# First batch of an attention and MLP kernel: squares in pairs, an earlier first k, and the last chunks divided anew

## Chip, cores, metric

One core of a Trainium2 chip. The metric is device time in microseconds (us) of that core. The trace's span is shorter than the time: by 2.1 us in the kernel before (399.3 and 401.45 for its profiled run).

## The reference

```python
# q, k, v: (8 batches, 12 heads, 448, 64) f32
scores = scale * q @ k^T;  attn = maximum(scores, 0)**2 / 448;  a = attn @ v
x = a.transpose(0, 2, 1, 3).reshape(3584, 768)
h = x @ w_in                                    # 768 x 2048
out = (maximum(h, 0) + alpha * minimum(h, 0)) @ w_out   # 2048 x 768
```

Attention without a softmax, then an MLP. The engines are called PE (TensorE, matmuls), DVE (VectorE), ACT (ScalarE) and POOL (GpSimd); PSUM is where this kernel's matmuls put their results. The kernel takes four heads at a time as a group: 24 groups n, three to a batch, each in 7 chunks j of scores.

## The kernel before

A chunk has score matmuls into PSUM (tile sc, two halves of one tile; or sch, two tiles), a relu to bf16 (rl) and a square on DVE (at). Attention times v (av) needs all 7 chunks of its group; its result is evicted to xT. The MLP runs as 16 ff chunks of 6 "hps" matmuls, an ACT and a DVE operation that writes gT, then "ops" matmuls with w_out. Batch 0 runs ahead of everything; from there the attention of later batches is spread between the MLP's matmuls, so that PE has no gap.

```python
for n in range(NG):                      # batch 0
    last = n == NG - 1
    for j in range(NJ):
        if j == 2 or (j == 5 and not last): scores(n, j, "both", mm_ps)
        else: scores(n, j, "both" if j == 6 and last else "act")
        squares(keep=1)
        if j == 2 and n > 0: attnv(n - 1, space=mm_ps)
        if j == 3 and not last: transpose(n + 1, "k")
        if j == 4 and not last: transpose(n + 1, "q")
        if last and j >= 4: ffn1(0, j - 4, range(0, 4))
    if n == 0:                           # the load queue, issued from POOL
        load_bf16(2)                     # k, q, v of group 2
        load_w_in(0, 512); load_w_in(512, 1024); load_w_in(1024, 2048)
        load_bf16(3)
# ... half of w_out, group 4, half of w_out ...
attnv(2, range(0, 4)); ffn1(0, 3, range(0, 4)); squares(both=True); attnv(2, range(4, NJ))
# ... beta from alpha ...
for ff in range(4): ffn1(0, ff, range(4, KM))
play([f[4], f[5], turn(3), f[6], f[7], (3, 0), f[8], ...])  # f[i]: ff chunk i; turn(3): transposes of k and q of group 3
```

```python
def group(units, phase):                 # the stream: up to three chunks of later groups
    def f():
        # ... scores of each unit, attnv ...
        squares()
        for n, j in units_:
            # ... at j == 0: load(n + 2), transpose k and q of n + 1 ...
            if j == 4 and n + 2 < NQ:
                for w in "kqv": to_bf16(n + 2, w, nc.gpsimd)   # POOL casts f32 -> bf16
    return f
```

## Time and profile before

| | before |
|---|---|
| time, four runs | 401.09 us median (400.79 to 401.98) |
| PE busy, share of the chain | 97%, 92% |
| start of the fifth ff chunk ("f4") | 33.68 us |
| transposes of q of group 3, landing of that q | 36.45 us, 34.93 us |
| first ops matmul | 50.54 us |

PE is nearly always busy, so one reads where it is not: ahead of f4. The prediction shows those lines. One more view: the loads that POOL issues. It is the issue list, cut to the issue of q of group 3; the last number is us from issue to landing.

```profile
qe<-in_q_dram POOLq DMA_DIRECT2D x1, 224.0 KB, 11.1
```

### The profile page before, as it was taken

The numbers are of one execution on the slowest core, as the hardware profiler recorded it, in microseconds if no ns is written. First come the engines' busy times: TensorE is split into PE (matmuls) and PEld (weight loads), VectorE is DVE, ScalarE is ACT, GpSimd is POOL, SyncE is SP. The second block draws the span as 40 slices with busy tenths as digits, with TensorE's granted clock in tenths as the row PEclk, the third lists the DMA queues.
The fourth block names the chain that finished last, engine by engine and source line by source line (L and its number), as shares of the span: only waits on it lengthen the run. The fifth ranks groups of instructions, "written<-read, shape, count | busy, mean of one in ns | idle before, by whom it ended". The sixth has DMA issues, their size and how long they took to land.

```text
span 399.3 us, 7923 instructions
## 1 busy us (share of the span) xinstructions
PE 387.3 (97%) x3201; PEld 200.8 (50%) x3201; DVE 258.1 (65%) x411; ACT 221.0 (55%) x345; POOL 72.8 (18%) x88
## 2 busy tenths in 40 slices
PE   8788999999999999999999999999999999999995
PEld 5434455444555445544555455554555445555562
DVE  3775767768664877567665777768575776736411
ACT  5785754788544766456544775656464585624200
POOL 6564000022021430033020360033002300000000
PEclk9699999999999999999999999999999999999999
DMA  6999995494098933393097961295058720130033
GB/s 145 189 209 205 203 250 204 116 242 150 21 244 202 252 136 80 86 270 100 2 215 197 250 192 43 64 274 155 2 144 187 200 48 0 41 79 2 0 80 79
DMA packets 64164, 55.44 MB, mean 139 GB/s; under 512 B 35696, under 2 KB 59776, under 8 KB 64128
## 3 DMA queue, kind: packets, MB, share of 16 engines
q1 hardware_dynamic: 53152, 44.98, 43.7%
q0 software_dynamic: 10976, 9.96, 15.6%
q8 instruction: 25, 0.41, 0.4%
q14 instruction: 11, 0.09, 0.1%
HBM read 45.62 MB, written 11.01 MB: 142 GB/s over the span
## 4 chain that ended last, share of the span: by engine, by line
PE 92%; DVE 2%; DMA 2%; ACT 1%; issue 1%; POOL 0%; ACTq 0%
PE ops L247 38%; PE hps L231 35%; PE av L202 7%; PE sc L159 6%; PE sch L159 4%; DMA qe<-in_q_dram 2%; DVE at L184 1%; PE tps L134 1%; DMA qraw<-in_q_dram 1%; PE avh L202 1%; ACT rl L173 0%; DVE gT L239 0%; ACT xT L211 0%; ACT xT L217 0%; POOL ke L103 0%
## 5 line engine op out<-in xcount | busy, mean ns | idle before, releaser
L247 PE MATMUL ops<-w_out_sb,gT 128*128 128x384 bf16 x896 | 153.4, 327 | 0.0
L231 PE MATMUL hps<-xT,w_in_sb 128*128 128x448 bf16 x768 | 151.2, 353 | 1.4 <-ACT xT L211 0.5
L184 DVE TENSOR_TENSOR at<-rl 128x896 bf16<-128x896 bf16 x167 | 111.1, 685 | 19.0 <-ACT rl L173 8.8
L247 PEld LDWEIGHTS <-gT 128*128 128x128 bf16 x896 | 84.1, 98 | 67.2 <-issue 14.7
L231 PEld LDWEIGHTS <-w_in_sb 128*128 128x128 bf16 x768 | 73.1, 98 | 75.7 <-issue 10.2
L239 DVE SCALAR_TENSOR_TENSOR gT<-neg,beta_sb,hps 128x448 bf16<-128x448 f32 x128 | 83.9, 677 | 35.7 <-ACT neg L238 35.1
L173 ACT ACTIVATE rl<-sc 128x896 bf16<-128x896 f32 x109 | 95.8, 927 | 7.7 <-PE sc L159 5.3
L238 ACT ACTIVATE neg<-hps 128x448 f32<-128x448 f32 x128 | 68.4, 553 | 55.0 <-PE hps L231 52.9
L255 DVE COPY osb<-ops 128x384 f32<-128x384 f32 x56 | 31.1, 555 | 54.5 <-PE ops L247 54.5
L109 POOL CAST kb<-kraw 128x896 bf16<-128x896 f32 x16 | 16.2, 1011 | 210.0 <-DMA kraw<-in_k_dram 210.0
L165 ACT ACTIVATE rl<-sch 128x448 bf16<-128x448 f32 x37 | 20.1, 544 | 56.4 <-PE sch L159 56.4
L159 PE MATMUL sc<-qT,kT 64*64 64x448 bf16 x464 | 36.4, 362 | 2.7 <-ACT rl L173 2.2
L202 PE MATMUL av<-at,vb 64*64 64x448 bf16 x616 | 33.1, 350 | 0.0
L166 DVE TENSOR_SCALAR rl<-sch 128x448 bf16<-128x448 f32 x37 | 23.0, 620 | 14.1 <-PE sch L159 14.1
L159 PEld LDWEIGHTS <-kT 64*64 64x64 bf16 x672 | 14.9, 106 | 29.6 <-issue 25.0
L202 PEld LDWEIGHTS <-vb 64*64 64x64 bf16 x672 | 20.3, 110 | 13.2 <-issue 1.4
L169 ACT ACTIVATE rl<-sch 128x448 bf16<-128x448 f32 x30 | 14.6, 544 | 16.9 <-PE sch L159 16.9
L217 ACT ACTIVATE xT<-av 128x896 bf16<-128x896 f32 x21 | 19.4, 922 | 6.8 <-PE av L202 6.7
L159 PE MATMUL sch<-qT,kT 64*64 64x448 bf16 x208 | 20.3, 380 | 0.0
L109 POOL CAST qb<-qraw 128x896 bf16<-128x896 f32 x16 | 18.4, 1151 | 0.0
L109 POOL CAST vb<-vraw 128x896 bf16<-128x896 f32 x16 | 16.8, 1053 | 1.4 <-DMA vraw<-in_v_dram 0.8
L171 DVE TENSOR_SCALAR rl<-sc 128x896 bf16<-128x896 f32 x6 | 6.5, 1084 | 2.9 <-PE sc L159 2.9
(47 smaller groups left out, 72.6 us busy)
## 6 DMA issues: line engine op xcount, KB each, us to landing
out_dram<-osb SPq DMA_DIRECT2D x56, 192.0 KB, 2.8
qraw<-in_q_dram SPq DMA_DIRECT2D x19, 448.0 KB, 4.6
kraw<-in_k_dram SPq DMA_DIRECT2D x19, 448.0 KB, 5.3
vraw<-in_v_dram SPq DMA_DIRECT2D x18, 448.0 KB, 6.3
w_out_sb<-in_moe_w_out_dram POOLq DMA_DIRECT2D x2, 1536.0 KB, 19.8
w_in_sb<-in_moe_w_in_dram POOLq DMA_DIRECT2D x8, 192.0 KB, 8.2
w_in_sb<-in_moe_w_in_dram POOLq DMA_DIRECT2D x4, 384.0 KB, 9.7
vb<-in_v_dram POOLq DMA_DIRECT2D x6, 224.0 KB, 9.9
```

Of the source, the lines that this page charges most:

```text
L109: eng.tensor_copy(o, i)
L159: nc.tensor.matmul(half[r][64 * c:64 * c + 64, :S], kT[n][64 * r:64 * r + 64, j, c, :], qT[n][64 * r:64 * r + 64, :, c, :], start=True, st ...
L165: nc.scalar.activation(rl[:, 0], half[0][:, :S], ACTF.Relu)
L166: nc.vector.tensor_scalar(rl[:, 1], half[1][:, :S], 0.0, None, ALU.max)
L173: nc.scalar.activation(rl, ps[:, :, :S], ACTF.Relu)
L184: nc.vector.tensor_tensor(a, rl, rl, ALU.mult)
L202: nc.tensor.matmul(half[r][64 * s:64 * s + 64, :S], vb[n][64 * r:64 * r + 64, s, j, :], a[64 * r:64 * r + 64, s], start=(j == 0), stop=(j ...
L231: nc.tensor.matmul(ps, w_in_sb[:, km // 2, km % 2, bass.ts(ff, 128)], xT[b][:, km // 2, km % 2, :], start=(km == 0), stop=(km == KM - 1))
L238: nc.scalar.activation(neg, ps, ACTF.Relu, scale=-1.0)
L239: nc.vector.scalar_tensor_tensor(gT[b // 2][:, ff, (b % 2) * S:(b % 2) * S + S], neg, beta_sb[:, ff:ff + 1], ps, ALU.mult, ALU.add)
L247: nc.tensor.matmul(ps, gT[sb][:, ff, bass.ts(c, 128)], w_out_sb[:, ff, bass.ts(hf, 384)], start=(ff == 0), stop=(ff == KF - 1))
L255: nc.vector.tensor_copy(o[:, bass.ts(hf, 384)], ps)
```

## The change

The intent is to start the dense stream sooner: fewer DVE operations in batch 0, first scores earlier, and a tail in which ACT and DVE work side by side.

```diff
-    g_pool = pool("g", 2)
+    g_pool = pool("g", 1)                    # makes room for the pair tiles
+    def squares2(keep=0):                    # one DVE operation on two chunks (128x1792)
+        while len(todo) >= 2 + keep: ...
+            nc.vector.tensor_tensor(a, t, t, ALU.mult)
@@ attention times v
+            elif apart:                      # two PSUM tiles, not two halves of one
+                av_ps[n] = [sc_ps.tile([128, 2, 512], ...)[:, 0] for _ in range(2)]
-            if g == NG - 1:
+            if g > 0:                        # second half of xT on DVE for groups 1 and 2
@@ first loads: k in two transfers
+    for js in (first, rest):                 # chunks 0-2, then 3-6
+        nc.sync.dma_start(out=raw[(0, "k")][:, :, lo:hi]..., in_=...)
-    warm(4)
     transpose(0, "k", first, nc.scalar)
     warm(2)
+    scores(0, 0, pair=True); scores(0, 1, pair=True); scores(0, 2, "both", mm_ps, pair=True)
     transpose(0, "k", rest)
@@ chunk loop
-                scores(n, j, "both" if j == 6 and last else "act")
+                scores(n, j, "dve" if last and j == 4 else "act", pair=True)
-            squares(keep=1)
+                squares2(keep=1)
@@ tail
-    attnv(2, range(0, 4)); ffn1(0, 3, range(0, 4)); squares(both=True); attnv(2, range(4, NJ))
+    squares(eng=nc.scalar)                   # the last chunk alone, on ACT
+    attnv(2, range(0, 4), apart=True); attnv(2, range(4, NJ)); ffn1(0, 3, range(0, 4))
```

The turning of alpha into beta also moves from the tail to the end of group 0.

More of the change, by code (lines that the diff above doesn't have):

```diff
@@ L59 @@
     at_pool = pool("at", 10)
+    rl2_pool = pool("rl2", 3)
+    at2_pool = pool("at2", 6)
     xT_pool = pool("xT", 2)
-    g_pool = pool("g", 2)
+    g_pool = pool("g", 1)
     neg_pool = pool("neg", 3)
@@ L148, with score_tile, score_mm @@
     att, xT, todo = {}, {}, []
-    def scores(n, j, relu="act", space=sc_ps):
+    def score_tile(space=sc_ps):
         if space is mm_ps:
-            half = [mm_ps.tile([128, 512], F32, tag="mm", name="sch") for _ in range(2)]
-        else:
-            ps = sc_ps.tile([128, 2, 512], F32, tag="sc", name="sc")
-            half = [ps[:, r] for r in range(2)]
-        for r in range(2):
+            return None, [mm_ps.tile([128, 512], F32, tag="mm", name="sch") for _ in range(2)]
+        ps = sc_ps.tile([128, 2, 512], F32, tag="sc", name="sc")
+        return ps, [ps[:, r] for r in range(2)]
+    def score_mm(n, j, half, rs=range(2)):
+        for r in rs:
             for c in range(2):
@@ L162, in scores, with relu_half, relu_tile @@
                                  start=True, stop=True)
-        rl = rl_pool.tile([128, 2, S], BF16, tag="rl", name="rl")
-        if relu == "both":
-            nc.scalar.activation(rl[:, 0], half[0][:, :S], ACTF.Relu)
-            nc.vector.tensor_scalar(rl[:, 1], half[1][:, :S], 0.0, None, ALU.max)
-        elif relu == "act2":
-            for r in range(2):
-                nc.scalar.activation(rl[:, r], half[r][:, :S], ACTF.Relu)
+    def relu_half(rl, half, r, eng):
+        if eng is nc.scalar:
+            nc.scalar.activation(rl[:, r], half[r][:, :S], ACTF.Relu)
+        else:
+            nc.vector.tensor_scalar(rl[:, r], half[r][:, :S], 0.0, None, ALU.max)
+    rl2, pairs = [], []
+    def relu_tile(pair):
+        if not pair:
+            return rl_pool.tile([128, 2, S], BF16, tag="rl", name="rl")
+        if not rl2:
+            t = rl2_pool.tile([128, 2, 2, S], BF16, tag="rl2", name="rlp")
+            rl2.extend([t, t])
+            pairs.append(t)
+        t = rl2.pop()
+        return t[:, 1 - len(rl2)]
+    def scores(n, j, relu="act", space=sc_ps, pair=False):
+        ps, half = score_tile(space)
+        score_mm(n, j, half)
+        rl = relu_tile(pair)
+        if relu in ("both", "act2"):
+            relu_half(rl, half, 0, nc.scalar)
+            relu_half(rl, half, 1, nc.vector if relu == "both" else nc.scalar)
         elif relu == "dve":
@@ L174, in scores, with squares @@
         todo.append((n, j, rl))
-    def squares(keep=0, both=False):
+    def squares2(keep=0):
+        while len(todo) >= 2 + keep:
+            two = [todo.pop(0) for _ in range(2)]
+            t = pairs.pop(0)
+            a = at2_pool.tile([128, 2, 2, S], BF16, tag="at2", name="atp")
+            nc.vector.tensor_tensor(a, t, t, ALU.mult)
+            for i, (n, j, _) in enumerate(two):
+                att[(n, j)] = a[:, i]
+    def squares(keep=0, eng=None):
         while len(todo) > keep:
@@ L179, in squares @@
             a = at_pool.tile([128, 2, S], BF16, tag="at", name="at")
-            if both:
-                nc.scalar.activation(a[:, 0], rl[:, 0], ACTF.Square)
-                nc.vector.tensor_tensor(a[:, 1], rl[:, 1], rl[:, 1], ALU.mult)
+            if eng is nc.scalar:
+                nc.scalar.activation(a, rl, ACTF.Square)
             else:
@@ L187, with attnv @@
     av_ps = {}
-    def attnv(n, js=range(NJ), space=sc_ps):
+    def attnv(n, js=range(NJ), space=sc_ps, apart=False):
         b, g = quads[n]
@@ L193, in attnv @@
                 av_ps[n] = [mm_ps.tile([128, 512], F32, tag="mm", name="avh") for _ in range(2)]
+            elif apart:
+                av_ps[n] = [sc_ps.tile([128, 2, 512], F32, tag="sc", name="av2")[:, 0] for _ in range(2)]
             else:
@@ L196, in attnv @@
         ps = av_ps[n]
-        half = ps if space is mm_ps else [ps[:, r] for r in range(2)]
+        half = ps if isinstance(ps, list) else [ps[:, r] for r in range(2)]
         for j in js:
@@ L311 @@
         raw[(0, w)] = raw_pool.tile([128, 2, NJ, D], F32, tag=w, name=f"{w}raw")
-        nc.sync.dma_start(out=raw[(0, w)].rearrange("p s j d -> p s (j d)"), in_=flat(0, w))
         cast[(0, w)] = early_pool.tile([128, 2, NJ, D], BF16, tag=w, name=f"{w}e")
+    first, rest = range(0, 3), range(3, NJ)
+    nc.sync.dma_start(out=raw[(0, "q")].rearrange("p s j d -> p s (j d)"), in_=flat(0, "q"))
+    for js in (first, rest):
+        lo, hi = js[0], js[-1] + 1
+        nc.sync.dma_start(out=raw[(0, "k")][:, :, lo:hi].rearrange("p s j d -> p s (j d)"),
+                          in_=flat(0, "k")[:, :, lo * D:hi * D])
     nc.sync.dma_start(out=alpha_sb, in_=moe_alpha.rearrange("(kf p) -> kf p", p=128))
@@ L324 @@
     transpose(0, "q")
-    first, rest = range(0, 3), range(3, NJ)
     nc.scalar.copy(cast[(0, "k")][:, :, :3], raw[(0, "k")][:, :, :3])
-    nc.vector.tensor_copy(cast[(0, "k")][:, :, 3:], raw[(0, "k")][:, :, 3:])
-    warm(4)
     transpose(0, "k", first, nc.scalar)
     warm(2)
+    nc.vector.tensor_copy(cast[(0, "k")][:, :, 3:], raw[(0, "k")][:, :, 3:])
+    scores(0, 0, pair=True)
+    scores(0, 1, pair=True)
+    scores(0, 2, "both", mm_ps, pair=True)
     transpose(0, "k", rest)
+    squares2(keep=1)
     for n in range(NG):
@@ L334 @@
         for j in range(NJ):
-            if j == 2 or (j == 5 and not last):
-                scores(n, j, "both", mm_ps)
-            else:
-                scores(n, j, "both" if j == 6 and last else "act")
-            squares(keep=1)
+            if n == 0 and j < 3:
+                continue
+            if last and j == 6:
+                scores(n, j)
+                squares2()
+            elif j == 5 and not last or j == 2:
+                scores(n, j, "both", mm_ps, pair=True)
+            else:
+                scores(n, j, "dve" if last and j == 4 else "act", pair=True)
+            if not (last and j == 6):
+                squares2(keep=1)
             if j == 2 and n > 0:
@@ L348 @@
         if n == 0:
+            ps = mm_ps.tile([128, KF], F32, tag="mm", name="aps")
+            nc.tensor.transpose(ps, alpha_sb, ident_f)
+            nc.vector.tensor_scalar(beta_sb, ps, -1.0, 1.0, ALU.mult, ALU.add)
             load_bf16(2)
@@ L356 @@
     nc.gpsimd.dma_start(out=w_out_sb[:, :, 384:], in_=w_out_v[:, :, 384:])
-    attnv(2, range(0, 4))
+    squares(eng=nc.scalar)
+    attnv(2, range(0, 4), apart=True)
+    attnv(2, range(4, NJ))
     ffn1(0, 3, range(0, 4))
-    squares(both=True)
-    attnv(2, range(4, NJ))
-    ps = sc_ps.tile([128, 2, 512], F32, tag="sc", name="aps")
-    nc.tensor.transpose(ps[:, 0, :KF], alpha_sb, ident_f)
-    nc.vector.tensor_scalar(beta_sb, ps[:, 0, :KF], -1.0, 1.0, ALU.mult, ALU.add)
     def turn(n):
```

## The prediction

> **What bounds the kernel now.** I read the page's busy shares and its chain first, then the chain in order of time for the first 75 us, then the timeline and one-microsecond stretches there.
>
> ```profile
> PE 387.3 (97%) x3201; PEld 200.8 (50%) x3201; DVE 258.1 (65%) x411; ACT 221.0 (55%) x345; POOL 72.8 (18%) x88
> ...
> PE ops L247 38%; PE hps L231 35%; PE av L202 7%; PE sc L159 6%; PE sch L159 4%; DMA qe<-in_q_dram 2%; DVE at L184 1%; PE tps L134 1%; DMA qraw<-in_q_dram 1%; PE avh L202 1%; ACT rl L173 0%; DVE gT L239 0%; ACT xT L211 0%; ACT xT L217 0%; POOL ke L103 0%
> ```
>
> TensorE carries 92% of the chain. The change touches only batch 0 (three groups n = 0, 1, 2) and the hand-over to the first full layer, so what counts is when the dense stream starts. In order of time:
>
> ```profile
> 5.52 6.09 DMA qe<-in_q_dram
> ...
> 15.14 2.61 PE avh L202 x26
> ...
> 30.73 0.55 ACT xT L211
> 31.28 0.02 issue
> 31.30 0.64 DVE xT L213
> ...
> 32.37 0.55 ACT neg L238
> 32.92 0.02 issue
> 32.94 0.69 DVE gT L239
> 33.63 0.04 issue
> 33.68 2.43 PE hps L231 x12
> ```
>
> From 33.68 us on the chain is nearly all PE; from there to 110 us the list of PE's waits holds two of 0.2 us. So the gain is the distance by which the matmul block now at 33.68 (the fifth ff chunk, "f4") moves forward. Ahead of it stand a DMA until 11.61 (q of group 1), then ACT and DVE alternating, then one serial tail. The timeline of the tail:
>
> ```profile
> 27.43 0.54 ACT L165 ACTIVATE rl<-sc 128x448 bf16<-128x448 f32 x1
> 28.00 0.62 DVE L166 TENSOR_SCALAR rl<-sc 128x448 bf16<-128x448 f32 x1 [0.77 <-ACT rl L165]
> ...
> 30.73 0.54 ACT L211 ACTIVATE xT<-av 128x448 bf16<-128x448 f32 x1 [2.15 <-PE av L202]
> ...
> 31.30 0.62 DVE L213 TENSOR_SCALAR xT<-av 128x448 bf16<-128x448 f32 x1 [1.84 <-ACT xT L211]
> ```
>
> Both pairs are meant to run side by side, yet DVE starts only when ACT ends. Each time both read halves of one PSUM tile (sc, av). Where the halves are tiles of their own (sch) they do overlap: ACT at 12.78 and DVE at 12.82. One more thing, from the one-microsecond stretches (columns: start:end, length, busy PE, PEld, DVE, ACT, POOL, then the clock):
>
> ```profile
> 10.00:11.00 1.00, 0.00 (x0) 0.00 (x0) 1.00 (x3) 1.00 (x2) 1.00 (x2) 1.00 1.02 128
> 11.00:12.00 1.00, 0.34 (x12) 0.35 (x14) 0.88 (x2) 0.42 (x1) 0.32 (x2) 1.00 1.08 152
> 12.00:13.00 1.00, 1.00 (x22) 0.30 (x17) 0.72 (x2) 0.22 (x1) 0.53 (x1) 0.60 1.21 187
> 13.00:14.00 1.00, 0.55 (x8) 0.13 (x5) 1.00 (x3) 1.00 (x2) 0.63 (x1) 0.50 1.26 202
> ```
>
> PE starves until that DMA lands and then runs at half clock from about 12.3 to 19.05 us: attention times v of group 0 takes 2.87 us there, of group 1 at full clock 1.52.
>
> **What the skill says.**
> - "TensorE: Matmul & The Clock Gate", Part 1: the clock is judged over a free-running window of about 3.4 us, half clock after an idle one. The trace agrees in length: half clock for 6.8 us, two windows. As the window runs free, where it falls can differ from run to run.
> - "VectorE: DVE Perf Modes", the perf-mode tier table: a bf16 tensor_tensor of 2048 takes 1224 ns, which is 2 elements a cycle (1067 ns) plus about 157 ns. For 896 that gives 624 ns; the trace has 618 (0.57 back to back).
> - "ScalarE: Activation LUTs", What ACT_TABLE_LOAD costs: 186 ns + 0.833 ns an element, so 932 for 896; the trace has 937 for relu here.
> - "DMA: Bandwidth & Descriptors", Issuing engines are not separate DMA queues: all transfers share 16 engines. In the trace the DMA share is 0.8 or more from 6 to 65 us, so work that comes earlier does not make data come earlier.
>
> **The change part by part.**
>
> *Three chunks of k ahead (before 11.6 us).* The first score matmul is at 7.21 us, after k lands at 5.17, four warm-up matmuls and the k copy. A smaller first k transfer and no warm-ups should bring it to about 6.6. But next PE needs k of group 1 (issued 4.68, 4.0 to landing: 8.7) and q of group 1 (5.52 + 6.1 = 11.6). Those two loads hang on q of group 0 landing at 3.9, which is unchanged. So PE waits from about 9.7 instead of 9.8. On the path: 0.
>
> *From 11.65 to about 17.8.* PE runs transposes, scores and group 0's attention times v at half clock and sets the pace; DVE stands idle from 17.25 to 19.06. Cheaper squares save nothing here. The alpha transpose (0.23 us) moves into a stretch where PE waits for ACT. Gain 0.
>
> *Squares in pairs.* From the trace 448 wide takes 0.384 and 896 0.618, so 1792 should take 0.618 + 2 x 0.234 = 1.09, back to back about 1.05. Against 2 x 0.57 that saves 0.1 us a pair; ten pairs save about 1 us of DVE. The price is that a square waits for the second relu.
>
> *Shifts between ACT and DVE.* ACT is busy nearly all of 17.8 to 28.0. It loses half of group 1's xT (0.56) and relu (2,4) (0.87), and the 0.3 us it waited for a square; it gains a whole relu and a whole square of the last chunk (0.87 + 0.93 instead of 0.54 + 0.58). DVE gains 0.62 and 1.08, loses the last half relu 0.62 and square 0.38. DVE from 19.06: two copies 1.25, two half relus 1.22, five pairs 5.25, xT half 0.62, relu (2,4) 1.08 = 9.4 us, so its last square ends at 28.6 with hardly a gap; before it was 29.46. Walking the order through with these durations, group 1's second xT half lands on DVE behind a paired square, at 25.5 (before 24.96 on ACT), and the last scores come at about 27.1 (before 26.99). ACT's relief is used up by DVE's load: gain to here 0.
>
> *The tail.* From scores at 27.45 done: relu on ACT to 28.4, its square to 29.3; attention times v needs both PSUM tiles, so starts at 28.45; its 28 matmuls end at about 30.1 (before 30.67), because the four hps matmuls that stood inside now follow and lie under the xT evictions. The evictions read two tiles, so run side by side: 30.15 to 30.75 (before 31.92). First hps complete 31.5, neg 0.55, gT 0.69, f4 at 32.85 against 33.68. **Gain 0.8 us.**
>
> *g in one buffer.* A pair of batches is written only after the last ffn2 of the pair before has run on the in-order PE, six hps matmuls earlier. Cost 0.
>
> Sum: 0 + 0 + 0 + 0.8. At best the paired squares give some tenths more, and I take **1.2 us**: 401.2 - 1.2 = **400.0 us**.
>
> **Rivals.**
> 1. *The half clock is avoided or falls elsewhere.* Group 0's attention times v would then end about 1.3 us earlier (2.87 against 1.52). For it: the window runs free, and PE's order is new. Against: the 1.9 us hole before q of group 1 stays. Then the tail could be 2.1 us early, but the next data stop it: q of group 3 is issued at 23.80 and lands 11.1 later, at 34.9, while its transposes now start at 36.45. With a saturated queue that caps the gain at about 1.5 us: 399.7, or 399 if the queue also runs a little ahead.
> 2. *DVE becomes the bound in group 2.* 9.4 us of work with no slack; a paired square in front of a relu or xT costs up to 1 us each. For it: DVE is at 5.00 of 5.00 between 20 and 25 us already. If two such waits land on the path, gain 0 or a loss of 0.5: 401 to 401.7.
> 3. *The front pays after all*, if the smaller k transfer lets the loads of group 1 in sooner. Those start at 6 us, after all of q and k is in. Perhaps 0.3 us: 399.7.
>
> **Range and chances.** The three runs of before spread over 1.2 us, and rivals 1 and 2 stand about 1 us to either side: 398.6 to 401.3. Two per cent is 8 us, while everything ahead of the stream lasts 33.7 us and PE idles about 7 us of the first 36, most of it waiting for first loads that stay. Faster by over 2%: 0.01; within: 0.98; slower: 0.01.
>
> **What will show it.** Right: q of group 1 lands near 11.6 and PE still waits for it; paired squares of 1.05 to 1.09 us; the two last xT evictions overlap; f4 at 32.3 to 33.2; PE without waits after it. Wrong, if f4 comes before 32 (then look at the clock from 12 to 19 us, and at q of group 3), if DVE waits put the last scores behind 28 us, or if gT writes wait for ffn2 at the start of batches 2, 4 and 6.

## The result

Ratios are the mean time of one kernel's fast runs over that of the other's of the same rounds, so not quite the ratio of the medians quoted. 401.49 us median of four runs (400.65 to 401.75) against 401.09: ratio 1.0003, 95% interval 0.9981 to 1.0024. That is the same time, and the gain of 1.2 us that I had taken as the point is not there. In the profile of the changed kernel nearly every step of batch 0 came true, most of them with more gain than I had worked out.

The row of the paired squares on the page:

```profile
L205 DVE TENSOR_TENSOR atp<-rlp 128x1792 bf16<-128x1792 bf16 x10 | 10.8, 1089 | 1.0 <-ACT rlp L196 0.8
```

The timeline of the tail (L245 and L247 are the two evictions to xT):

```profile
29.45 0.54 ACT L245 ACTIVATE xT<-av 128x448 bf16<-128x448 f32 x1 [0.46 <-PE av L236]
29.61 0.62 DVE L247 TENSOR_SCALAR xT<-av 128x448 bf16<-128x448 f32 x1 [1.46 <-PE av L236]
...
32.16 2.43 PE L265 MATMUL hps<-xT,w_in_sb 128*128 128x448 bf16 x12 [0.21 <-DVE gT L273]
```

A pair costs 1089 ns, the two evictions overlap, and f4 starts at 32.16 (forecast: 32.3 to 33.2), which is 1.52 us earlier than before. By the "lead" of a trace I mean below how much earlier the same matmul starts in it than in the traced kernel before. Next comes the chain of the changed kernel:

```profile
23.82 0.40 PE sc L161 x8
24.22 0.02 issue
24.24 11.13 DMA qe<-in_q_dram
35.38 0.04 issue
35.42 0.58 PE tps L136 x14
36.00 2.38 PE hps L265 x12
...
126.73 0.21 issue
126.95 0.55 ACT rl L168
127.52 3.81 DVE at L216 x3
131.32 0.60 DVE gT L273
...
220.56 3.78 DVE at L216 x3
```

The chain no longer runs through batch 0's tail: from 24.24 to 35.38 us it is the landing of q of group 3. PE waits for it, and of the lead of 1.52 us 1.01 is left. It is still 1.01 at 126 us. Then two stretches appear that the chain of before had not: three DVE squares and a gT write, at the start of batches 2 and 4. There the lead falls to 0.3 us, and then turns into a lag of 0.3 to 0.4. (At the start of batch 6, at 313 us, both chains have such a stretch.) So of the 1.52 us the load took 0.5 and the stream 1.4, and the two profiled runs took the same time, 401.49 and 401.45, as 0.3 us of the lag come back outside the span. The same place in the two timelines, before first:

```profile
127.80 0.93 POOL L109 CAST kb<-kraw 128x896 bf16<-128x896 f32 x1 [9.69 <-DMA kraw<-in_k_dram]
128.53 3.21 DVE L184 TENSOR_TENSOR at<-rl 128x896 bf16<-128x896 bf16 x3 [0.76 <-ACT rl L169]
128.67 1.32 POOL L109 CAST qb<-qraw 128x896 bf16<-128x896 f32 x1
129.94 1.32 POOL L109 CAST vb<-vraw 128x896 bf16<-128x896 f32 x1
```

```profile
127.38 0.93 POOL L111 CAST kb<-kraw 128x896 bf16<-128x896 f32 x1 [9.11 <-DMA kraw<-in_k_dram]
127.52 3.81 DVE L216 TENSOR_TENSOR at<-rl 128x896 bf16<-128x896 bf16 x3 [0.76 <-ACT rl L168]
128.25 1.33 POOL L111 CAST qb<-qraw 128x896 bf16<-128x896 f32 x1
129.53 1.32 POOL L111 CAST vb<-vraw 128x896 bf16<-128x896 f32 x1
...
131.97 0.54 PE L265 MATMUL hps<-xT,w_in_sb 128*128 128x448 bf16 x2 [0.47 <-DVE gT L273]
```

In the second column are durations. Three squares should take 3 x 0.62. Beside POOL's casts they take 3.21 in one kernel and 3.81 in the other, and in the changed one PE then waits 0.47 us for gT. The casts start when a DMA lands, the squares when PE has made scores; a lead of 1 us shifts the one against the other. Over the whole trace of before, the 140 squares of 896 with no cast beside them took 611 to 627 ns, and the 14 that lay wholly beside casts took 1086 on average (changed kernel: 16, 1179).

### The profile page after: what moved, and what is told of

Read it like the earlier page. It is cut to its first block, busy times and chain, and to the rows that moved or that the text cites. A ratio compares the mean times of both kernels' runs of the same rounds, so it can differ in the third digit from the quotient of the medians.

```text
span 399.7 us, 7892 instructions
## 1 busy us (share of the span) xinstructions
PE 386.3 (97%) x3197; PEld 200.5 (50%) x3197; DVE 261.6 (65%) x401; ACT 220.6 (55%) x343; POOL 73.4 (18%) x88
## 4 chain that ended last, share of the span: by engine, by line
PE 87%; DMA 5%; DVE 3%; ACT 2%; issue 1%; POOL 0%; ACTq 0%
PE ops L281 38%; PE hps L265 32%; PE av L236 7%; PE sc L161 5%; DMA qe<-in_q_dram 4%; PE sch L161 4%; DVE at L216 3%; PE avh L236 1%; PE tps L136 1%; DMA qraw<-in_q_dram 1%; ACT rlp L196 1%; DVE gT L273 0%; ACT rl L168 0%; ACT xT L251 0%; POOL ke L105 0%
## 5 line engine op out<-in xcount | busy, mean ns | idle before, releaser
L216 DVE TENSOR_TENSOR at<-rl 128x896 bf16<-128x896 bf16 x147 | 102.9, 721 | 16.7 <-ACT rl L196 6.8
L265 PEld LDWEIGHTS <-w_in_sb 128*128 128x128 bf16 x768 | 73.0, 98 | 76.3 <-issue 11.6
L196 ACT ACTIVATE rl<-sc 128x896 bf16<-128x896 f32 x95 | 83.6, 924 | 7.2 <-PE sc L161 5.0
L168 ACT ACTIVATE rl<-sch 128x448 bf16<-128x448 f32 x62 | 32.0, 543 | 71.9 <-PE sch L161 71.9
L111 POOL CAST kb<-kraw 128x896 bf16<-128x896 f32 x16 | 15.4, 962 | 210.3 <-DMA kraw<-in_k_dram 202.8
L236 PE MATMUL av<-at,vb 64*64 64x448 bf16 x592 | 32.0, 349 | 0.0
L161 PEld LDWEIGHTS <-kT 64*64 64x64 bf16 x672 | 14.7, 106 | 29.1 <-issue 24.6
L170 DVE TENSOR_SCALAR rl<-sch 128x448 bf16<-128x448 f32 x32 | 19.9, 621 | 13.9 <-PE sch L161 13.9
L111 POOL CAST vb<-vraw 128x896 bf16<-128x896 f32 x16 | 18.3, 1143 | 0.5 <-DMA vraw<-in_v_dram 0.5
L196 ACT ACTIVATE rlp<-sc 128x896 bf16<-128x896 f32 x14 | 12.3, 933 | 1.7 <-PE sc L161 1.7
L205 DVE TENSOR_TENSOR atp<-rlp 128x1792 bf16<-128x1792 bf16 x10 | 10.8, 1089 | 1.0 <-ACT rlp L196 0.8
```

Of the source, the lines that this page charges most:

```text
L111: eng.tensor_copy(o, i)
L161: nc.tensor.matmul(half[r][64 * c:64 * c + 64, :S], kT[n][64 * r:64 * r + 64, j, c, :], qT[n][64 * r:64 * r + 64, :, c, :], start=True, st ...
L168: nc.scalar.activation(rl[:, r], half[r][:, :S], ACTF.Relu)
L170: nc.vector.tensor_scalar(rl[:, r], half[r][:, :S], 0.0, None, ALU.max)
L196: nc.scalar.activation(rl, ps[:, :, :S], ACTF.Relu)
L216: nc.vector.tensor_tensor(a, rl, rl, ALU.mult)
```

## The experiments

Twelve kernels in three jobs, each five rounds; all gave correct results. Each job ran on a chip of its own, so ratios are within a job, and kernels of different jobs are compared through the kernel before. The kernel before had medians of 401.85, 401.17 and 401.18 us there (11 runs each, 399.6 to 403.3 in all), so single times scatter by more than what is looked for. Ratios against it:

| kernel | median us (six runs) | ratio, 95% interval | f4 in its trace |
|---|---|---|---|
| g_one | 401.66 | 0.9997 (0.9984 to 1.0009) | 31.88 |
| after_sep | 400.34 | 0.9959 (0.9941 to 0.9978) | 29.14 |
| after_sh9 | 402.47 | 1.0025 (0.9994 to 1.0056) | 29.68 |
| after_q3 | 398.80 | 0.9933 (0.9912 to 0.9954) | 29.27 |
| after_again | 401.91 | 1.0010 (0.9973 to 1.0048) | 29.67 |
| before_sep | 400.43 | 0.9987 (0.9957 to 1.0017) | 31.93 |
| after_order | 398.43 | 0.9929 (0.9901 to 0.9957) | 29.23 |
| before_order | 399.97 | 0.9979 (0.9946 to 1.0012) | 31.29 |
| after_order_sep | 399.05 | 0.9940 (0.9910 to 0.9970) | 29.53 |
| before_order_sep | 400.52 | 0.9976 (0.9951 to 1.0002) | 33.06 |
| before_order_tail | 400.11 | 0.9972 (0.9949 to 0.9995) | 30.88 |
| after_order_front | 398.83 | 0.9938 (0.9914 to 0.9962) | 30.44 |

**First job.** My theory A was the collision of squares and casts; rival B the single buffer for g; rival C scatter. (A kernel with two buffers in the changed kernel does not fit into memory, so B was tried the other way round.)

g_one, the kernel before with one buffer:

```diff
-    g_pool = pool("g", 2)
+    g_pool = pool("g", 1)
```

> The kernel before with one buffer for g instead of two, nothing else. Theory A (the one buffer is innocent; the changed kernel gives its gain back because DVE squares run beside POOL casts at 127 and 220 us): same time as before, within 0.3 us (401.1), no PE gap of 0.4 us at the start of batches 2, 4 and 6 beyond those of before. Rival B (gT writes wait for the one buffer): PE gaps of about 0.5 us at the start of batches 2 and 4, time up by 0.6 to 1.3 us (401.7 to 402.4).

Ratio 0.9997: the one buffer costs nothing, and rival B falls. But this trace held a surprise. Its batch 0 is that of before, and yet f4 came at 31.88 instead of 33.68: q of group 1 had landed at 10.5 us instead of 11.6, and after it first reached full clock PE did not fall back to half. The front is not the same from run to run.

after_sep, the changed kernel with held casts:

```diff
+            if after is not None: nc.gpsimd.tensor_copy(t[:, 0, 0, 0:1], after)
@@ in the stream (att[ends] is the last square of the group)
-                        to_bf16(n + 2, w, nc.gpsimd)
+                        to_bf16(n + 2, w, nc.gpsimd, att[ends][:, 0, 0:1] if w == "k" else None)
```

> The changed kernel, but the POOL casts of a group wait until the group's last square is done (a one-column copy from the square's result ahead of the first cast). Theory A: squares in the stream take 0.62 us each even at 127 and 220 us, the PE gaps there vanish, the lead of 1.0 us that the changed kernel has at 50 us stays to the end: about 400.2. Rival B (one buffer) or rival C (the loss is scatter between runs): gaps and time as in the changed kernel, 401.3 to 401.6.

Ratio 0.9959, and in the trace the stretch at 128 us is clean:

```profile
128.42 0.63 DVE L218 TENSOR_TENSOR at<-rl 128x896 bf16<-128x896 bf16 x1 [0.76 <-ACT rl L170]
129.23 0.63 DVE L218 TENSOR_TENSOR at<-rl 128x896 bf16<-128x896 bf16 x1 [0.18 <-ACT rl L198]
130.04 0.62 DVE L218 TENSOR_TENSOR at<-rl 128x896 bf16<-128x896 bf16 x1 [0.18 <-ACT rl L198]
...
130.73 0.19 POOL L123 COPY kb<-at 128x1 bf16<-128x1 bf16 x1 [8.03 <-DVE at L218]
```

So the collision is real. The ratio is against the kernel before; the changed kernel itself did not run in this job. And that the median comes near the expected 400.2 is in part luck, for the lead of this trace at 50 us was not 1.0 us, it was 0.11, although f4 came 4.54 us earlier than before. Its timeline and one-microsecond stretches show where that went:

```profile
33.55 0.58 PE L138 MATMUL tps<-ident,ke 128*64 128x128 bf16 x14 [1.98 <-DMA ke<-in_k_dram]
...
34.70 0.92 PE L138 MATMUL tps<-ident,qe 128*64 128x128 bf16 x14 [0.56 <-DMA qe<-in_q_dram]
```

```profile
34.00:35.00 1.00, 0.44 (x14) 0.31 (x10) 0.00 (x0) 0.82 (x1) 0.91 (x2) 0.89 1.27 200
35.00:36.00 1.00, 1.00 (x14) 0.61 (x11) 0.35 (x1) 0.08 (x1) 0.21 (x2) 0.50 1.32 205
36.00:37.00 1.00, 1.00 (x4) 0.35 (x3) 0.28 (x1) 0.00 (x0) 1.00 (x2) 0.50 1.30 202
```

PE arrives early, waits 2.5 us for k and q of group 3, falls to half clock (third number from the end: 0.50) for 3.4 us, and the lead is gone. This became theory D: up to 36 us the load queue that POOL issues sets the time.

after_sh9, the changed kernel delayed by about 1 us of empty matmuls:

```diff
-    play([..., turn(3), f[6], f[7], (3, 0), ...
+    play([..., turn(3), f[6], f[7], lambda: warm(9), (3, 0), ...
```

> The changed kernel with nine idle warm-up matmuls (about 1.0 us of PE) put in after the eighth ff chunk, so that the stream from there has the timing of the kernel before. Theory A: the squares at 127 and 220 us collide with the casts as little as in the kernel before, so the 1.0 us put in is not paid at the end: time 401.0 to 401.7, as the changed kernel or before. Rival B: the gaps stay and the 1.0 us is added: 402.4.

This is a miss for theory A as I had put it: ratio 1.0025 with an interval from 0.9994 to 1.0056 and one run of 406.0. The trace had PE gaps of 0.40 and 0.28 us at 132 and 226. It was no clean test: its f4 had come early, at 29.68, so with the delay it still led by 0.48 us from 50 to 126 us, and then lost 0.9 us by 150. Yet the trace of the next kernel, with a lead of 0.40 us there, lost nothing at that place. So the lead alone does not decide how squares and casts meet.

after_q3, group 3 ahead of the last load of w_in (its second half):

```diff
-            load_w_in(1024, 2048)
             load_bf16(3)
+            load_w_in(1024, 2048)
```

> The changed kernel with the loads of group 3 issued ahead of the last third of w_in. Theory A: the wait of PE for q of group 3 at 35.4 us (0.3 to 0.5 us) vanishes, the lead at 50 us is 1.5 us instead of 1.0; what of it is left at the end depends on how squares and casts meet: 400.2 to 401.2. If the third part of w_in now comes too late, PE waits for it near 38 us and the lead is smaller than 1.0.

Ratio 0.9933, more than expected. In the trace, the slowest of its six runs (401.1), PE no longer waited for group 3 but for w_in, 0.76 us at 36.1 and 1.34 at 37.8: the same queue.

**Second job.** Theory D against A alone. In it the loads were put in the order in which PE asks for them, in both kernels.

after_again is the changed kernel itself.

> The changed kernel unchanged, for more of its runs beside those of the others. All theories: within 0.3% of before. Theory D (the load queue issued from POOL sets the time up to 36 us): whenever f4 (the fifth ff chunk) comes, the transposes of q of group 3 end between 35.4 and 36.3 us, and the lead over before at 50 us is between 0 and 1.1 us.

Ratio 1.0010. The traced run had f4 at 29.67, 4.0 us ahead, and q of group 3 turned at 34.93, as soon as it had landed; 1.5 us were left at 50 us, which is 0.4 more than the largest lead I had expected. This trace had no gap at 132 or 225 and ended 1.8 us ahead of the traced run of before, yet other runs of the six took up to 403.45.

before_sep holds the casts in the kernel before.

> The kernel before with the POOL casts of the stream held until the group's last square. If the meeting of squares and casts costs the kernel before as well, it gains 0.5 to 1.2 us here, and what the same edit gave the changed kernel (1.6 us against before) is mostly no merit of the change. If before was free of that cost (its trace has no PE gap at 127 and 220 us), it gains under 0.3 us.

Ratio 0.9987, its interval contains 1. This decides nothing: 0.13% is 0.5 us, the lower end of the first case of the expectation, and the interval reaches from no gain to the 0.4% of after_sep. The trace speaks for a cost in before as well: its lead over the traced run of before grew from 1.66 us at 50 us to 2.19 at the end.

after_order and before_order:

```diff
-            load_w_in(1024, 2048)
-            load_bf16(3)
+            load_bf16(3, "kq")
+            load_w_in(1024, 1536)
+            load_w_in(1536, 2048)
@@
     nc.gpsimd.dma_start(out=w_out_sb[:, :, :384], in_=w_out_v[:, :, :384])
+    load_bf16(3, "v")
```

> The changed kernel with the load queue in the order of use: k and q of group 3 ahead of the last half of w_in, that half in two pieces, v of group 3 behind the first half of w_out. Theory D: PE no longer waits for a load between f4 and the first ops matmul; the lead at 50 us over the traced kernel before is as large as that of f4, 1.5 us (q of group 1 late) to 4.5 us (early); time 1 to 3.5 us below before. If PE's order and not the loads bounds this stretch: at most 1 us below before.

> The kernel before with the same order of loads. Theory D: it gains too, since its f4 comes between 30.5 and 33.7 us and is held up by the same loads when early; but it stays 1.0 to 1.6 us behind the changed kernel with that order, which is what the change of batch 0 is worth once the loads do not hide it. If the change is worth nothing in itself: no difference between the two.

0.9929 and 0.9979. Theory D holds, and this is the main result. The chain of after_order:

```profile
29.23 2.43 PE hps L265 x12
31.66 0.90 PE tps L136 x28
32.56 2.38 PE hps L265 x12
34.94 0.31 PE sc L161 x4
```

f4, both transposes and the next ff chunks follow without a wait. The lead at 50 us over the traced run of before is 4.45 us, equal to that of f4; in before_order it is 2.39, again equal to that of f4. Both had q of group 1 early (9.95 and 10.34) and full clock from 4.4 us on. At 50 us the two differ by 2.06 us. The mean times of the six runs differ by 1.99 (398.34 and 400.33; 95% about 1.3 either way), which is what the change is worth in time when the loads do not hide it. That the two figures agree is luck: 0.3 of the 1.99 lie outside the span, and the trace of after_order lost 1.2 us again beside the casts, with PE gaps of 0.58 at 128.6 and 0.44 at 221.7, so that at their ends the two traces differ by 1.14. In the kernel before, the new order alone gives 0.2% that cannot be told from nothing.

**Third job.** Both edits together, and the change in parts.

> The changed kernel with the loads in order of use and the POOL casts of the stream held back. Both theories hold: lead over the traced kernel before of 4.4 us at 50 us if q of group 1 lands by 10.5 us (1.5 if it lands near 11.7), and no PE gap over 0.3 us at 128 and 221 us, so that the lead stays: 396.5 to 397.5 where before has 401.2, the fastest of all kernels here. If the held casts only move the collision elsewhere: as with the order alone, 0.7% below before.

> The kernel before with both edits. Its stream had hardly a gap to remove, so 0.2 to 0.5% below before, and 1.5 to 2.5 us behind the changed kernel with both edits: that is what the change of batch 0 is worth when neither the loads nor the collisions take it back. If the two edits carry all of the gain: no difference between them.

0.9940 and 0.9976. The traced run of after_order_sep, at full clock, kept its lead of 4.15 us and ended 4.73 us ahead (span 394.6), with no gap but the 0.16 us that all kernels have. But four of its six runs had a mean clock of 0.991 to 0.995 and took 398.7 to 399.8, so in time it is not faster than after_order, and a part of the expectation failed: 396.5 to 397.5 was reached in two runs only. That the held casts help once the loads are in order is thus shown in the trace and not in the times. All four traces with held casts agree: from 50 us to 335 us each gains 0.54 us on the traced run of before, while the nine other traces of this table and of the changed kernel come out between 1.4 lost and 0.25 gained. A part of it is paid back outside the span: time less span is 2.2 us in after_order_sep against 1.8 in after_order, and 2.5 against 2.1 in before_order_sep and before_order. The two kernels with both edits differ by 1.82 us in the mean (398.55 and 400.37; 95% about 1.4 either way), which confirms the worth of the change a second time. The trace of before_order_sep fell to half clock from 10.85 us on, so that attention times v of group 0 took 2.87 us instead of 1.66 in before_order: most of why its f4 is late.

before_order_tail has the tail edits of the change (above) in before_order:

> The kernel before with the loads in order of use and only the tail of the change (two PSUM tiles for the last attention times v, its hps matmuls after it, last relu and square whole on ACT). The stretch from the last scores to f4, which was 6.68 us in all traces of before and 5.50 in all of the changed kernel, is 5.5 to 5.8; f4 comes 1.0 to 1.2 us earlier than in the kernel before with that order (31.3), at about 30.2; time 0.2 to 0.5% below before. If the tail needs the other parts: above 6.3.

The stretch from the last scores to f4 was 6.68 us in every trace of a kernel with the old tail, 5.50 in every one of the changed kernel, and 5.77 here. In the traces the tail is worth 0.9 us by itself and 1.2 with the rest; in time it does not show, 0.9972 here and 0.9979 for before_order. f4 itself was later than expected (30.88), as the first scores came at 7.47 instead of 6.97.

after_order_front undoes the k part in after_order: one transfer, four warm-up matmuls, all of k turned first.

> The changed kernel with the loads in order of use but k of group 0 loaded and turned as in the kernel before (one transfer, four warm-up matmuls, all of k turned before the first scores). As predicted: the k part is worth nothing, since q of group 1 is waited for in either case; f4 within 0.3 us of the changed kernel with that order (29.2) when q of group 1 lands at 10.0 to 10.5. If the front counts once q of group 1 lands early: f4 at 29.6 to 30.2.

f4 at 30.44 against 29.23 and 29.53 with the part. So the front counts once q of group 1 lands at 10 us. The 0.9 to 1.2 us are not cleanly separated: the first scores came at 7.68 here, but PE's clock also rose later, at 6.03 us, against 4.39 and 5.38. The traces of after_again and after_sh9, which have the k part, had q of group 1 at 9.9 and 9.7 us and a clock that rose later still, at 6.45 and 6.47; their first scores came at 6.91 and f4 at 29.67 and 29.68. That leaves 0.8 us for the k part. The ratio, 0.9938, is within the interval of after_order.

## Why the prediction was right in kind and wrong in its sum

"Within 2%" held. On the median of 401.23 that the prediction began from, the ratio of 1.0003 makes 401.35, just above the upper edge of the range (401.3); the point was 1.35 us too low, and the reasons are partly others than I wrote. In the two traces the sum is: f4 earlier by 1.52 us; 0.5 lost to the landing of q of group 3; 1.4 lost beside the casts; 0.1 regained; 0.3 gained outside the span.

1. **"From 33.68 us on the chain is nearly all PE ... So the gain is the distance by which [f4] moves forward."** This step failed. What moves f4 moves the end only as far as the loads allow: over the traces with the old queue f4 lay anywhere from 29.1 to 33.7, and the transposes of q of group 3 from 34.7 to 36.5. I had listed that limit under rival 1, as a cap on a lucky case. It was in force in the ordinary case, and tighter than 1.5 us, for q of group 3 itself landed 0.45 us later (35.38). And the second loss, beside the casts, I had not listed at all (point 6). I had read a trace in which PE came late and no wait showed, and took the missing wait for room.
2. **The front, "On the path: 0", and "q of group 1 lands near 11.6".** True of the two traces compared first (11.61 and 11.68), but in the twelve others with a trace it landed between 9.7 and 10.9. What sets the landing is not known: the twelve ran on three chips, and the record does not name the chip of the first two. With the earlier landing the k part is worth 0.8 us, hidden by the queue unless the loads are reordered. The moved turning of alpha, "Gain 0", then has a price: in after_order PE waits 0.59 us at 13.7 for the beta operation, which DVE runs behind a paired square (0.81 and 0.86 in after_order_sep and after_order_front). Whether that moves f4 was not tested.
3. **The tail, 0.8 us by the walk.** Right in kind, small in size: the stretch from the last scores to f4 shrank by 1.18, and the last scores came at 26.66 where I had 27.1.
4. **Paired squares of 1.05 to 1.09 us; g in one buffer at no cost.** Both right: 1089 ns, and 0.9997 for g_one.
5. **Rival 1, the half clock.** The clock matters, but the hole I knew is not the only one: a faster front lengthens PE's wait for group 3 and can throttle it there (after_sep, 34.78 to 38.19 us). With loads in order, the runs of the changed kernel's three variants averaged 397.8 us where the mean clock was 0.996 or more (8 runs) and 399.2 below it (10 runs); those of the kernel before 401.1 (21 runs) and 402.0 (12 runs).
6. **The stream after f4 as neutral to a shift.** Not foreseen. A lead moves DVE's squares against POOL's casts, and in the trace of the changed kernel 1.2 us of PE's lead went at 127 to 132 and 220 to 225 us, and 0.2 more by 140 and 232. Holding the casts kept the lead in all four traces that have it. In time it gave 0.4% in one comparison, against the kernel before and not the changed one, and nothing that can be told in three others.

The prediction missed a page that bears on 6: the Trainium skill, "SBUF — State Buffer", Who interferes with whom, says that a DVE instruction with two SBUF inputs contends with a GpSimd instruction that reads SBUF, the later one waiting. The traces agree that both sides are slowed: a square takes 623 ns alone and 1.1 to 1.2 us on average beside casts, a cast 0.93 us alone and up to 1.35 there.

Left open: why q of group 1 lands at 10 or at 11.6 us, and why single runs of both kernels scatter from 399.3 to 403.5 (the clock goes with about 1 us of it). The changed kernel with the order alone (398.43) or with the casts held as well (399.05) beats both kernels by 0.6 to 0.7%; between the two the runs do not decide.

## What to carry to other kernels

Before a stretch is shortened, list what the next stage needs from elsewhere and when it lands, also where no wait shows: slack of 1.5 us is a cap of 1.5 us at most (here 1.0, as the landing moved as well). An early stage that is hidden behind a load queue is worth its time only together with the queue's order; here each alone gave 0 to 0.2% and both 0.7%. And compare more than one trace of each kernel before explaining a difference of a microsecond, since f4 of one and the same program, the changed kernel, came at 32.16 in one trace and at 29.67 in another.

## What the Trainium skill lacked or had wrong

- "VectorE: DVE Perf Modes", the tier table: the rate of tensor_tensor holds (1089 ns measured for 1792 wide, 1090 estimated by its terms), but the table has no word on a GpSimd operation beside it, which made a square of 623 ns take up to 1407. That stands on "SBUF — State Buffer", as said above.
- "TensorE: Matmul & The Clock Gate", Part 1: the half clock lasted 6.83 us (two of its windows) or 3.41 (one), as the page has it. But the window before was not an idle one, as the page's table says: in the kernel before PE was busy for 1.56 us of the 3.40 from 8.8 to 12.2 us, and half clock followed. The page says that the ramp's cost is under 1% of a kernel; the runs with loads in order differed by 1.4 us of 398 with the clock, so that holds, but it was as large as what was looked for.
- "DMA: Bandwidth & Descriptors" has no rate for a load that casts on its way. Here the POOL-issued casting loads moved 200 to 210 GB/s from 13 to 53 us with the engines' share at 1.2 to 1.3, against 377 to 394 for the plain first loads of q and k. The two are not the same count: the profile counts a casting load by the bf16 that it writes (224 KB for 448 KB of f32). By what is read, an estimate is twice that, some 400 to 420 GB/s, so these loads were not slower.
